# Weight decoding on 513 columns as 27 rows of 19, each VectorE step between touching and gapped rows

## The chip, the cores and the metric

The kernel runs on one core of one Trainium2 chip. The metric is the device time of one execution in microseconds; the figure given for a kernel is the median of its runs. The core has TensorE (PE, with its weight loads shown apart as PEld), VectorE (DVE), ScalarE (ACT), GpSimd (POOL) and SyncE (SP), which issues the transfers here.

## What is computed

The reference is an attention over 4 batches of 8 heads (576 positions, 64 wide) that keeps only the scores within tau of the row's maximum, and then two feed-forward layers on its 2304 x 512 output. The weights of both layers come as float64; they are 512 x 2048 and 2048 x 512.

```python
def _attn_ref(q, k, v, tau):
    scores = scale * np.matmul(q, k.transpose(0, 1, 3, 2))
    thresh = np.max(scores, axis=-1, keepdims=True) - tau
    scores = np.where(scores >= thresh, scores, -1000000000.0)
    scores = scores - np.max(scores, axis=-1, keepdims=True)
    attn = np.exp(scores)
    attn = attn / (np.sum(attn, axis=-1, keepdims=True) + 1e-09)
    return np.matmul(attn, v).astype(np.float32)

def _moe_ref(x, w_in, w_out, alpha):
    h = x @ w_in
    g = np.maximum(h, 0.0) + alpha * np.minimum(h, 0.0)
    return (g @ w_out).astype(np.float32)

def _moe2_ref(x, w_in, w_out):
    h = x @ w_in
    g = h * np.clip(h + 3.0, 0.0, 6.0) / 6.0
    return (g @ w_out).astype(np.float32)
```

## The kernel before, in words

**Attention.** A loop of 144 steps (16 pairs of heads, 9 steps each) runs `do_S` (scores on PE, L361, into the PSUM tile `s`), `soft` (row maximum on DVE, L382; exponential on ACT, L383; threshold and sum on DVE, L385), `soft_norm` (division on POOL, L394), `do_T` (transposes on PE) and `do_PV`. Beside it `prep` splits and transposes the next pair's q and k (`nat`, L102 and L103).

**Feed-forward.** `ffn_groups` makes, for a block of 512 tokens, sixteen `h_group`s (PE L199 into `h`; the nonlinearity in `act1` on DVE L204 and L207, or `act2` on ACT L213 and DVE L215; the high and low part of `g` on ACT L221 and POOL L225) and sixteen `o_group`s (PE L229 or L235, added up on DVE in L487 or L489). Three of the four blocks are queued and dealt out between the attention steps; the last block and a rest of 256 tokens follow at the end.

**Weights.** There are 64 weight chunks of 128 x 512 (16 each of `i1`, `o1`, `i2`, `o2`). Each one is decoded once, in the first block's passes, from float64 to float32, and stored to a scratch in DRAM, from which all later passes load it. A decode is: the load of 512 KB into `raw64` (L125, three buffers); on ACT, the low word scaled to 16 bits (L131, into every second 16-bit place of `low`) and the absolute value of the high word (L132, into `f`); on DVE, the sign and exponent bits taken from 16 bits of the high word (L133, from every fourth 16-bit place of `raw64` into the other places of `low`), a clamp (L135, `f` onto itself) and a shift by 3 (L136, `f` onto itself); on POOL, the sum of `f` and `low` (L137); the store (L138). Then `split` makes the high part on ACT (L102) and the low part on POOL or DVE (L103). Six chunks are decoded early, in the first pair's attention steps; the other 58 come when `ready` asks for them, one chunk ahead of the matmuls that use it.

**Order.** Every engine runs its own queue in order. The queues' order is set by the framework's scheduler when the program is built, from the order in the code, the priorities (`high_priority` for the attention steps) and its own estimates of durations. A change in the instructions can therefore move others.

Of the kernel before, what the change touches and what calls it, by code (L numbers as in the profile page):

```python
# [9 lines left out]
F32 = mybir.dt.float32  # L10
F32R = mybir.dt.float32r
U32 = mybir.dt.uint32
U16 = mybir.dt.uint16
AF = mybir.ActivationFunctionType
ALU = mybir.AluOpType
# [4 lines left out]
P = 128  # L20
NKT = 4


F64_LO = 2.0 ** -15
F64_HI = 122879.9921875


def f32(ap):
    return ap.bitcast(F32)
# [3 lines left out]
def kernel(  # L33
# [13 lines left out]
    nc = tc.nc  # L47
    B, H, S, D = q.shape
    DM = H * D
# [3 lines left out]
    SM = 512  # L53
# [23 lines left out]
    def pool(stack, name, bufs, **kw):  # L77
        return stack.enter_context(tc.tile_pool(name=name, bufs=bufs, **kw))

    const = pool(ctx, "const", 1)  # L80
    stage = pool(ctx, "stage", 4)
# [4 lines left out]
    dec = pool(ctx, "dec", 3)  # L86
# [14 lines left out]
    def split(hi, lo, src, lo_eng):  # L101
        nc.scalar.copy(hi, src)  # L102
        lo_eng.tensor_tensor(out=lo, in0=src, in1=f32(hi), op=ALU.subtract)  # L103
# [3 lines left out]
    wide = moe_w_in.dtype != F32  # L107
    scratch = {}
# [6 lines left out]
    def chunk(nm, ft):  # L115
        w = weights[nm]
        if nm[0] == "i":
            n = w.shape[1] // NF
            return w[:, ft * n:(ft + 1) * n].rearrange("(k p) f -> p k f", p=P)
        return w[ft * P:(ft + 1) * P, :]  # L120

    def decode_load(nm, ft):
        raw = dec.tile([P, DM, 2], U32, tag="raw", name="raw64")
        dst = raw.rearrange("p (k f) a -> p k (f a)", k=NKT) if nm[0] == "i" else raw.rearrange("p n a -> p (n a)")
        nc.sync.dma_start(dst, chunk(nm, ft))  # L125
        return raw

    def decode(nm, ft, raw):
        f = stage.tile([P, DM], U32, tag="st", name="f")
        low = dec.tile([P, DM, 2], U16, tag="low", name="low", bufs=2)  # L130
        nc.scalar.activation(low[:, :, 0], raw[:, :, 0], AF.Copy, scale=2.0 ** -29)  # L131
        nc.scalar.activation(f32(f), f32(raw[:, :, 1]), AF.Abs)  # L132
        nc.vector.tensor_scalar(out=low[:, :, 1], in0=raw.bitcast(U16)[:, :, 3], scalar1=0x8000, scalar2=0x4000,  # L133
                                op0=ALU.bitwise_and, op1=ALU.bitwise_xor)
        nc.vector.tensor_scalar(out=f32(f), in0=f32(f), scalar1=F64_HI, scalar2=F64_LO, op0=ALU.min, op1=ALU.max)  # L135
        nc.vector.tensor_single_scalar(f, f, 3, op=ALU.logical_shift_left)  # L136
        nc.gpsimd.tensor_tensor(out=f, in0=f, in1=low.bitcast(U32).rearrange("p n a -> p (n a)"), op=ALU.add)  # L137
        nc.sync.dma_start(scratch[nm, ft], f32(f))  # L138
        return f32(f)

    raws = {}

    def w_fetch(key, nm, ft, fresh=False):
        if key in raws:
            return
        if wide and fresh:
            raws[key] = decode_load(nm, ft)
            return
        t = stage.tile([P, DM], F32, tag="st", name="st")
        if wide:  # L150
            nc.sync.dma_start(t, scratch[nm, ft])
        elif nm[0] == "i":
            nc.sync.dma_start(t.rearrange("p (k f) -> p k f", k=NKT), chunk(nm, ft))
        else:
            nc.sync.dma_start(t, chunk(nm, ft))
        raws[key] = t
# [12 lines left out]
    def fetch(kind, c):  # L169
        if c < len(passes) * NF and (kind, c) not in ws:  # L170
            nm, ft, _, _, fresh = w_of(kind, c)
            w_fetch((kind, c), nm, ft, fresh)

    def ready(kind, c):
        if c < len(passes) * NF and (kind, c) not in ws:
            fetch(kind, c)
            nm, ft, layer, blk, fresh = w_of(kind, c)
            t = raws.pop((kind, c))
            if wide and fresh:
                t = decode(nm, ft, t)  # L180
            w = (wip if kind == "i" else wop).tile([P, 2, DM], F32R, tag="w" + kind, name="w" + kind)
            if fresh:
                on_dve = layer == 2 and ft % 4 == 3
            else:
                on_dve = ft % 4 < (1 if layer == 1 and blk is not None else 2)
            split(w[:, 0], w[:, 1], t, nc.vector if on_dve else nc.gpsimd)
            ws[kind, c] = w

    def load_x(t, src, n, lo_eng):
        for kt in range(NKT):  # L190
            raw = stage.tile([P, SM], F32, tag="st", name="st")
            nc.sync.dma_start(raw[:, :n], src[kt])
            split(t[:, 0, kt, :n], t[:, 1, kt, :n], raw[:, :n], lo_eng)
        return t
# [57 lines left out]
    for i in range(2):  # L252
        t = a1.tile([P, 2, P], F32R, tag=f"qr{i}", name=f"qr{i}")
# [5 lines left out]
    for i in range(2):  # L259
        t = a1.tile([P, 2, NB + 1, D], F32, tag=f"v{i}", name=f"v{i}")  # L260
# [9 lines left out]
    st = {}  # L270
# [175 lines left out]
    def x_ready(blk):  # L446
        if ("x", 1, blk) not in box:
            box["x", 1, blk] = x0 if blk == 0 else load_x(new_x(), x1d[blk], blocks[blk], nc.gpsimd)
# [73 lines left out]
    def decode_early(n):  # L522
        for nm, ft in early_dec[n - 1:n]:
            decode(nm, ft, raws.pop((nm, ft)))
            decoded.add((nm, ft))
        for nm, ft in early_dec[n:n + 1]:
            w_fetch((nm, ft), nm, ft, True)
# [26 lines left out]
    for i in range(NS):  # L554
        pi, t = divmod(i, NT)
# [4 lines left out]
        if t % 2 == 1 or t == NT - 1:  # L560
            with tc.high_priority(offset=50):
                n = 1 + t % 2
# [6 lines left out]
        while done < min(len(queue), (i + 1 - PB - LAG) * per):  # L569
            f, a = queue[done]  # L570
# [5 lines left out]
    for f, a in queue[done:]:  # L576
# [8 lines left out]
    NBR = blocks[B]  # L585
    LAGO = 2
    xs = {blk: load_x(x2p.tile([P, 2, NKT, blocks[blk]], F32R, tag=f"x{blk}", name="x"), x1d[blk], blocks[blk], nc.vector)
          for blk in (B - 1, B)}
    for layer in (1, 2):
# [6 lines left out]
        for m in range(len(seq) + LAGO):  # L596
            if m < len(seq):
                ft, blk = seq[m]
                n = blocks[blk]
# [11 lines left out]
            ft, blk = seq[m - LAGO]  # L611
            gs = gss.pop(m - LAGO)
            n = blocks[blk]
# [9 lines left out]
            else:  # L623
                for d in range((n + P - 1) // P):
                    o = oa[d] if blk < B else orr[d]
                    mm_o2(o, ws["o", c0 + ft], gs, d, n, first_, last_)
                    if last_:
                        t = ob.tile([P, SM], F32, tag="ob", name="ob")
# [38 lines left out]
```

## Time and profile before

| | us |
|---|---|
| median of 3 runs | 1209.13 (1207.42 to 1209.55) |
| the profiled execution, its own time | 1206.91 |
| span in its profile | 1205.1 |
| PE busy | 1133.9 (94% of the span) |
| POOL busy | 703.9 (58%) |
| DVE busy | 678.6 (56%) |
| ACT busy | 662.8 (55%) |

The profiled execution took 1.8 us more than the span of its profile: that much lies before the first and behind the last instruction. It is 2.2 us below the median of the runs. "Busy" counts the time in which an engine has an instruction under way; instructions of one engine that follow directly can overlap by a few hundredths of a microsecond in the records. Shares of the whole span hide that the stages have different limits, so the profile is best read by stretches of time.

### The profile page before, as it was taken

To read this page: it belongs to the slowest core of one execution; us is meant where nothing else is said; L and a number is where in the kernel's file an instruction comes from. 1 tells how busy PE (TensorE), PEld (TensorE's weight loads), DVE (VectorE), ACT (ScalarE), POOL (GpSimd) and SP (SyncE) were. 2 spreads that over 40 slices of the span, in tenths; PEclk is the share of its full clock that TensorE was granted. 3 is DMA by queue.
4 is the path that set the end of the run, shared out by engine and by line. 5 is a ranking of instruction groups with operands and counts; after the bars stand their busy time and mean duration, and the time that the engine had idled before them with its cause. 6 is when DMAs were issued, how large, how long until landed. Compare 5 with 4: busy or idle time off the path is not lost.

```text
span 1205.1 us, 19458 instructions
## 1 busy us (share of the span) xinstructions
PE 1133.9 (94%) x6944; PEld 939.0 (78%) x6944; DVE 678.6 (56%) x1297; ACT 662.8 (55%) x1272; POOL 703.9 (58%) x710
## 2 busy tenths in 40 slices
PE   5899998888888999999999999999999999999998
PEld 4677786666667787878788878888777888888886
DVE  6877789979979563737254555555235333331221
ACT  6788776757777564546565545445534322243432
POOL 2775788977978775655555665545343443334332
PEclk9899999999899999999999999999999999999999
DMA  6852355475575443242333432232224322212211
GB/s 176 252 151 63 112 175 170 142 208 162 152 243 170 150 147 101 76 120 81 109 86 106 145 107 84 79 103 71 80 79 149 97 61 62 67 57 69 63 36 53
DMA packets 93634, 139.09 MB, mean 115 GB/s; under 512 B 19424, under 2 KB 48608, under 8 KB 93536
## 3 DMA queue, kind: packets, MB, share of 16 engines
q1 hardware_dynamic: 93536, 137.83, 38.9%
q8 instruction: 55, 0.90, 0.3%
q14 instruction: 43, 0.35, 0.1%
HBM read 103.29 MB, written 25.17 MB: 107 GB/s over the span
## 4 chain that ended last, share of the span: by engine, by line
PE 60%; DVE 3%; issue 1%; POOL 1%; DMA 1%; ACT 1%; DVEq 0%; POOLq 0%; ACTq 0%
PE h L199 25%; PE o L235 12%; PE o L229 11%; PE s L361 3%; PE pv L425 3%; PE t L407 2%; PE r L229 2%; PE r L235 2%; DMA st<-wo 1%; DVE m L204 1%; DVE g L207 1%; PE pt L306 1%; POOL wo L103 0%; DVE g L215 0%; PE r L410 0%
## 5 line engine op out<-in xcount | busy, mean ns | idle before, releaser
L199 PE MATMUL h<-x,wi 128*128 128x512 f32 (+1 forms) x1536 | 356.6, 381 | 2.9 <-DVE g L207 1.0
L225 POOL TENSOR_TENSOR gs<-g,gs 128x512 fp32r<-128x512 f32 (+1 forms) x160 | 194.6, 1217 | 220.0 <-ACT gs L221 218.9
L199 PEld LDWEIGHTS h<-x,wi 128*128 128x128 f32 x1536 | 273.7, 189 | 56.7 <-DVE g L207 1.5
L235 PE MATMUL o<-wo,gs 128*128 128x512 f32 x768 | 197.5, 402 | 10.0 <-DVE g L215 7.2
L229 PE MATMUL o<-gs,wo 128*128 128x512 f32 x768 | 196.1, 401 | 9.1 <-DVE g L207 8.1
L235 PEld LDWEIGHTS o<-wo,gs 128*128 128x128 f32 x768 | 142.3, 191 | 43.8 <-DVE g L215 9.8
L229 PEld LDWEIGHTS o<-gs,wo 128*128 128x128 f32 x768 | 141.9, 191 | 41.0 <-DVE g L207 11.7
L215 DVE SCALAR_TENSOR_TENSOR g<-m,h 128x512 f32<-128x512 f32 x80 | 50.3, 630 | 163.2 <-ACT m L213 161.9
L204 DVE TENSOR_SCALAR m<-h,alpha_sb 128x512 f32<-128x512 f32 x80 | 55.5, 694 | 145.8 <-PE h L199 145.6
L221 ACT CAST gs<-g 128x512 fp32r<-128x512 f32 (+1 forms) x160 | 92.8, 580 | 72.1 <-DVE g L207 34.6
L394 POOL TENSOR_SCALAR e<-e,rc 128x576 f32<-128x576 f32 x144 | 116.6, 820 | 25.7 <-DVE rc L391 24.5
L383 ACT ACTIVATE e<-s,nmx 128x576 f32<-128x576 f32 x144 | 107.3, 749 | 43.7 <-DVE nmx L382 43.0
L385 DVE SCALAR_TENSOR_TENSOR e<-s,thr,e 128x576 f32<-128x576 f32 x144 | 115.9, 811 | 18.4 <-ACT e L383 15.1
L382 DVE TENSOR_REDUCE nmx<-s 128x1 f32<-128x576 f32 x144 | 107.2, 750 | 31.6 <-PE s L361 31.2
L103 POOL TENSOR_TENSOR wi<-st,wi 128x512 fp32r<-128x512 f32 x58 | 74.8, 1290 | 79.6 <-ACT wi L102 79.4
L425 PE MATMUL pv<-p,v 128*64 128x128 f32 (+1 forms) x1600 | 109.7, 273 | 9.3 <-DVE g L215 6.7
L361 PE MATMUL s<-ka,qt 128*128 128x288 f32 x512 | 101.1, 323 | 17.0 <-DVE e L385 9.5
L213 ACT ACTIVATE m<-h,three 128x512 f32<-128x512 f32 x80 | 51.3, 644 | 116.1 <-PE h L199 115.8
L102 ACT CAST wo<-st 128x512 fp32r<-128x512 f32 x99 | 59.3, 622 | 91.8 <-DMA st<-wo 75.9
L425 PEld LDWEIGHTS pv<-p,v 128*64 128x64 f32 x1600 | 84.8, 139 | 31.8 <-issue 15.1
L103 POOL TENSOR_TENSOR wo<-st,wo 128x512 fp32r<-128x512 f32 x58 | 77.2, 1347 | 50.7 <-ACT wo L102 50.5
L102 ACT CAST wi<-st 128x512 fp32r<-128x512 f32 x99 | 60.9, 616 | 80.3 <-PE h L199 43.6
(85 smaller groups left out, 1648.8 us busy)
## 6 DMA issues: line engine op xcount, KB each, us to landing
st<-wi SPq DMA_DIRECT2D x99, 256.0 KB, 2.7
st<-wo SPq DMA_DIRECT2D x99, 256.0 KB, 2.7
raw<-in_moe_w_in_dram SPq DMA_DIRECT2D x32, 512.0 KB, 4.4
raw<-in_moe_w_out_dram SPq DMA_DIRECT2D x32, 512.0 KB, 4.0
ka<-ka SPq DMA_DIRECT2D x30, 304.0 KB, 4.3
wi<-f SPq DMA_DIRECT2D x32, 256.0 KB, 3.1
wo<-f SPq DMA_DIRECT2D x32, 256.0 KB, 3.1
raw<-in_k_dram SPq DMA_DIRECT2D x16, 256.0 KB, 3.6
```

The costliest lines, as they stand in the source:

```text
L102: nc.scalar.copy(hi, src)
L103: lo_eng.tensor_tensor(out=lo, in0=src, in1=f32(hi), op=ALU.subtract)
L199: nc.tensor.matmul(h[:, :n], lhsT=w[:, ws, kt * P:(kt + 1) * P], rhs=x[:, xs, kt, :n], start=(i == 0), stop=(i == len(steps) - 1))
L225: nc.gpsimd.tensor_tensor(out=gs[:, 1, :n], in0=g[:, :n], in1=f32(gs[:, 0, :n]), op=ALU.subtract)
L229: nc.tensor.matmul(o[:, :n], lhsT=w[:, ws, dt * P:(dt + 1) * P], rhs=gs[:, gsel, :n], start=fresh and start and i == 0, stop=stop and i == ...
L235: nc.tensor.matmul(o[:m, :], lhsT=gs[:, gsel, tt * P:tt * P + m], rhs=w[:, ws, :], start=start and i == 0, stop=stop and i == 2)
L361: nc.tensor.matmul(ps[:, half, 0:SH], lhsT=w, rhs=s["k"][:, a, c + half * SH:c + half * SH + SH], start=(n == 0), stop=(n == len(mms) - 1))
L382: nc.vector.tensor_reduce(out=nmx, in_=ps, axis=AX.XY, op=ALU.max, negate=True)
L383: nc.scalar.activation(eh, ps, AF.Exp, bias=nmx, scale=1.0)
L385: nc.vector.scalar_tensor_tensor(out=eh, in0=ps, scalar=thr, in1=eh, op0=ALU.is_ge, op1=ALU.mult, accum_out=sm[:, h:h + 1])
L394: nc.gpsimd.tensor_scalar(out=eh, in0=eh, scalar1=rc[:, h:h + 1], scalar2=0.0, op0=ALU.mult, op1=ALU.add)
L425: nc.tensor.matmul(pv[64 * h:64 * h + 64, :], lhsT=vn[:, h, kt, :], rhs=pt[:, blk, c:c + m], start=(kt == 0), stop=(kt == NB), skip_group_ ...
```

## The change

Each decode now works on 513 columns: the 512 of the chunk and one column of padding, seen as 27 rows of 19. The tiles `raw64` and `f` (and with it every tile of the pool `stage`) get 513 columns, in which the 27 rows touch. The tile `low` and a new tile `cl` get 540 columns, of which each row of 20 uses 19, so their rows have a gap. The three DVE steps each go from one kind to the other: L133 (now L151) from `raw64`, touching, to `low`, gapped; the clamp L135 (now L153) from `f`, touching, to `cl`, gapped, where it was from `f` to `f`; the shift L136 (now L154) from `cl`, gapped, back to `f`, touching. The framework writes the touching side as one run of 513. The ACT step L131 (now L149) writes gapped rows, and the POOL sum L137 (now L155) reads them from `low`. The three buffers of `raw64` are now made once, with the padding column set to zero by three small POOL instructions at the start, and taken in turn; transfers still move 512 columns.

```diff
--- before.py
+++ after.py
@@ -119,24 +119,43 @@
             return w[:, ft * n:(ft + 1) * n].rearrange("(k p) f -> p k f", p=P)
         return w[ft * P:(ft + 1) * P, :]
 
+
+
+    RA, RB, RG = 27, 19, 20
+    raw64 = []
+    for i in range(3 if wide else 0):
+        t = const.tile([P, RA * RB, 2], U32, name=f"raw64{i}")
+        nc.gpsimd.memset(t[:, DM:], 0)
+        raw64.append(t)
+
+    def rows(ap):
+        return ap.rearrange("p (a b) -> p a b", a=RA)[:, :, 0:RB]
+
+    def st_tile(dt, name):
+        return stage.tile([P, RA * RB], dt, tag="st", name=name)
+
     def decode_load(nm, ft):
-        raw = dec.tile([P, DM, 2], U32, tag="raw", name="raw64")
-        dst = raw.rearrange("p (k f) a -> p k (f a)", k=NKT) if nm[0] == "i" else raw.rearrange("p n a -> p (n a)")
+        raw = raw64.pop(0)
+        raw64.append(raw)
+        dst = raw[:, 0:DM]
+        dst = dst.rearrange("p (k f) a -> p k (f a)", k=NKT) if nm[0] == "i" else dst.rearrange("p n a -> p (n a)")
         nc.sync.dma_start(dst, chunk(nm, ft))
         return raw
 
     def decode(nm, ft, raw):
-        f = stage.tile([P, DM], U32, tag="st", name="f")
-        low = dec.tile([P, DM, 2], U16, tag="low", name="low", bufs=2)
-        nc.scalar.activation(low[:, :, 0], raw[:, :, 0], AF.Copy, scale=2.0 ** -29)
+        f = st_tile(U32, "f")
+        cl = dec.tile([P, RA * RG], U32, tag="cl", name="cl", bufs=2)
+        low = dec.tile([P, RA * RG, 2], U16, tag="low", name="low", bufs=2)
+        nc.scalar.activation(rows(low[:, :, 0]), rows(raw[:, :, 0]), AF.Copy, scale=2.0 ** -29)
         nc.scalar.activation(f32(f), f32(raw[:, :, 1]), AF.Abs)
-        nc.vector.tensor_scalar(out=low[:, :, 1], in0=raw.bitcast(U16)[:, :, 3], scalar1=0x8000, scalar2=0x4000,
+        nc.vector.tensor_scalar(out=rows(low[:, :, 1]), in0=rows(raw.bitcast(U16)[:, :, 3]), scalar1=0x8000, scalar2=0x4000,
                                 op0=ALU.bitwise_and, op1=ALU.bitwise_xor)
-        nc.vector.tensor_scalar(out=f32(f), in0=f32(f), scalar1=F64_HI, scalar2=F64_LO, op0=ALU.min, op1=ALU.max)
-        nc.vector.tensor_single_scalar(f, f, 3, op=ALU.logical_shift_left)
-        nc.gpsimd.tensor_tensor(out=f, in0=f, in1=low.bitcast(U32).rearrange("p n a -> p (n a)"), op=ALU.add)
-        nc.sync.dma_start(scratch[nm, ft], f32(f))
-        return f32(f)
+        nc.vector.tensor_scalar(out=rows(f32(cl)), in0=rows(f32(f)), scalar1=F64_HI, scalar2=F64_LO, op0=ALU.min, op1=ALU.max)
+        nc.vector.tensor_single_scalar(rows(f), rows(cl), 3, op=ALU.logical_shift_left)
+        nc.gpsimd.tensor_tensor(out=rows(f), in0=rows(f), in1=rows(low.bitcast(U32).rearrange("p n a -> p (n a)")), op=ALU.add)
+        f = f32(f)[:, 0:DM]
+        nc.sync.dma_start(scratch[nm, ft], f)
+        return f
 
     raws = {}
 
@@ -146,7 +165,7 @@
         if wide and fresh:
             raws[key] = decode_load(nm, ft)
             return
-        t = stage.tile([P, DM], F32, tag="st", name="st")
+        t = st_tile(F32, "st")[:, 0:DM]
         if wide:
             nc.sync.dma_start(t, scratch[nm, ft])
         elif nm[0] == "i":
@@ -188,7 +207,7 @@
 
     def load_x(t, src, n, lo_eng):
         for kt in range(NKT):
-            raw = stage.tile([P, SM], F32, tag="st", name="st")
+            raw = st_tile(F32, "st")[:, 0:SM]
             nc.sync.dma_start(raw[:, :n], src[kt])
             split(t[:, 0, kt, :n], t[:, 1, kt, :n], raw[:, :n], lo_eng)
         return t
```

The number of decode instructions on each engine stays the same; the scheduler puts some in another place. On DVE, in the stretch where blocks of the first layer run between attention steps, this is the decode of one chunk (`f_2810` before, `f_2815` now; `e`, `s`, `nmx`, `thr`, `rc` belong to the attention, `acc` to the feed-forward layer). Before:

```order
L385 SCALAR_TENSOR_TENSOR e_3557,sm_3558<-s_3666,thr_3672,e_3557 128x576
L385 SCALAR_TENSOR_TENSOR e_3790,sm_3791<-s_3785,thr_3793,e_3790 128x576
L135 TENSOR_SCALAR f_2810<-f_2810 128x512
L487 TENSOR_TENSOR acc_2041<-o_2679,acc_2041 128x512
L391 RECIPROCAL rc_3678<-den_3677 128x2
L136 TENSOR_SCALAR f_2810<-f_2810 128x512
```

And with the change:

```order
L153 TENSOR_SCALAR cl_2816<-f_2815 128x27x19
L404 SCALAR_TENSOR_TENSOR e_3563,sm_3564<-s_3672,thr_3678,e_3563 128x576
L154 TENSOR_SCALAR f_2815<-cl_2816 128x513
L404 SCALAR_TENSOR_TENSOR e_3796,sm_3797<-s_3791,thr_3799,e_3796 128x576
L410 RECIPROCAL rc_3684<-den_3683 128x2
L506 TENSOR_TENSOR acc_2047<-o_2685,acc_2047 128x512
```

The clamp and the shift now stand ahead of and between the two softmax steps instead of behind them.

On POOL, these are sums of early decodes and the work between them. Before:

```order
L137 TENSOR_TENSOR f_496<-f_496,low_497 128x512
L394 TENSOR_SCALAR e_438<-e_438,rc_463 128x576 x2
L137 TENSOR_TENSOR f_576<-f_576,low_577 128x512
L103 TENSOR_TENSOR nat_364<-raw_261,nat_364 128x9x64
L137 TENSOR_TENSOR f_651<-f_651,low_652 128x512
```

And with the change:

```order
L155 TENSOR_TENSOR f_501<-f_501,low_503 128x513
L409 TENSOR_SCALAR den_467<-sm_444 128x2
L103 TENSOR_TENSOR nat_369<-raw_267,nat_369 128x9x64
L155 TENSOR_TENSOR f_581<-f_581,low_583 128x513
L413 TENSOR_SCALAR e_443<-e_443,rc_468 128x576 x2
```

The sum and the division of the attention (L394, now L413) have changed places. Behind row 498 of some 1,440 on PE the order of the matmuls is that of before.

## Rows read from the trace of the kernel before

**Rows 1.** The page, part 1: busy time of PE over the whole span.

```profile
PE 1133.9 (94%) x6944; PEld 939.0 (78%) x6944; DVE 678.6 (56%) x1297; ACT 662.8 (55%) x1272; POOL 703.9 (58%) x710
```

**Rows 2.** Busy time by stretch: us, engines, clock granted to PE, DMA share, GB/s.

```profile
0.00:30.00 30.00, 17.73 (x99) 14.86 (x99) 20.15 (x54) 20.07 (x37) 8.74 (x18) 1.00 0.61 175
30.00:180.00 150.00, 140.38 (x1117) 113.89 (x1118) 119.72 (x276) 118.96 (x243) 113.29 (x140) 0.97 0.52 150
180.00:390.00 210.00, 175.88 (x1039) 142.30 (x1038) 186.82 (x304) 144.92 (x265) 174.35 (x153) 0.96 0.59 178
390.00:420.00 30.00, 28.30 (x160) 22.54 (x161) 16.93 (x28) 17.92 (x37) 23.36 (x22) 0.94 0.52 164
420.00:1205.00 785.00, 771.58 (x4532) 645.38 (x4530) 335.03 (x638) 360.88 (x695) 384.18 (x380) 1.00 0.30 88
```

**Rows 3.** PE's waits in 180 to 390 us: total, times, longest.

```profile
PE s L361 <- DVE e L385: 7.3, 4, 4.9
PE o L229 <- DVE g L207: 6.9, 4, 3.8
PE pv L425 <- DVE g L215: 6.7, 3, 4.6
PE s L361 <- DVE thr L384: 3.5, 1, 3.5
PE o L235 <- DVE g L215: 2.5, 2, 2.3
```

**Rows 4.** DVE's costliest groups in 180 to 390 us: busy us, mean ns.

```profile
L133 DVE TENSOR_SCALAR low<-raw 128x512 uint16<-128x512 uint16 x42 | 38.2, 910 | 3.9 <-POOL f L137 3.9
L136 DVE TENSOR_SCALAR f<-f 128x512 uint32<-128x512 uint32 x43 | 37.9, 881 | 0.5
L135 DVE TENSOR_SCALAR f<-f 128x512 f32<-128x512 f32 x43 | 36.8, 860 | 7.9 <-ACT f L132 7.9
```

**Rows 5.** The three DVE decode steps, whole run: duration ns min/median/max.

```profile
L133 DVE TENSOR_SCALAR low<-raw x64: 440/588/1659, 22.3 to 402.5; 128x512 uint16<-128x512 uint16 x64
...
L135 DVE TENSOR_SCALAR f<-f x64: 397/740/1720, 24.3 to 409.7; 128x512 f32<-128x512 f32 x64
...
L136 DVE TENSOR_SCALAR f<-f x64: 400/778/1532, 24.8 to 410.2; 128x512 uint32<-128x512 uint32 x64
```

**Rows 6.** DVE alone in order of time, 196 to 216 us: start, duration, instruction.

```profile
197.36 1.51 DVE L136 TENSOR_SCALAR f<-f 128x512 uint32<-128x512 uint32 x1
...
209.79 0.41 DVE L135 TENSOR_SCALAR f<-f 128x512 f32<-128x512 f32 x1
...
212.50 1.24 DVE L133 TENSOR_SCALAR low<-raw 128x512 uint16<-128x512 uint16 x1
```

**Rows 7.** POOL alone over the same time.

```profile
197.10 1.49 POOL L103 TENSOR_TENSOR nat<-raw,nat 128x576 fp32r<-128x576 f32 x1
...
210.89 1.27 POOL L137 TENSOR_TENSOR f<-f,low 128x512 uint32<-128x512 uint32 x1 [1.79 <-ACT low L131]
212.12 1.28 POOL L103 TENSOR_TENSOR wi<-f,wi 128x512 fp32r<-128x512 f32 x1
```

**Rows 8.** DVE steps with an operand in PSUM, 150 to 420 us: duration ns min/median/max.

```profile
L385 DVE SCALAR_TENSOR_TENSOR e<-s,thr,e x35: 792/804/820, 149.5 to 399.6; 128x576 f32<-128x576 f32 x35
...
L215 DVE SCALAR_TENSOR_TENSOR g<-m,h x15: 665/673/689, 300.2 to 418.6; 128x512 f32<-128x512 f32 x15
```

**Rows 9.** A DVE step of two operands in SBUF, whole run: duration ns min/median/max.

```profile
L103 DVE TENSOR_TENSOR wi<-st,wi x41: 666/684/830, 46.1 to 1161.6; 128x512 fp32r<-128x512 f32 x41
```

**Rows 10.** POOL's steps, whole run: duration ns min/median/max.

```profile
L103 POOL TENSOR_TENSOR nat<-raw,nat x30: 1402/1429/1627, 15.2 to 782.5; 128x576 fp32r<-128x576 f32 x30
...
L137 POOL TENSOR_TENSOR f<-f,low x64: 1259/1294/1482, 25.4 to 410.8; 128x512 uint32<-128x512 uint32 x64
...
L394 POOL TENSOR_SCALAR e<-e,rc x144: 741/752/1464, 18.0 to 846.9; 128x576 f32<-128x576 f32 x144
```

**Rows 11.** POOL's division of the attention in 180 to 390 us: busy us, mean ns.

```profile
L394 POOL TENSOR_SCALAR e<-e,rc 128x576 f32<-128x576 f32 x25 | 24.0, 968 | 3.6 <-DVE rc L391 3.5
```

## The prediction

> **What bounds the kernel now.** I read the page first, then the busy time by stretch, then PE's waits in the stretch that stood out, then the DVE steps that the change touches, one by one. Over the whole span PE is busy 94% [rows 1], which looks like a kernel that only PE can shorten. The stretches say more [rows 2]. From 420 us on PE is busy 771.58 of 785 us: nothing that DVE or POOL saves there can be worth more than 13 us, and no decode runs there at all, since the last one starts at 410 us [rows 5]. Between 180 and 390 us PE is busy only 175.88 of 210 us, while DVE is busy 186.82 (89%) and POOL 174.35 (83%). In this stretch 43 of the 64 chunks are decoded [rows 4], and the waits of PE name DVE: the five longest sums come to 7.3 + 6.9 + 6.7 + 3.5 + 2.5 = 26.9 us of PE's 34.1 us of idle time [rows 3], 79%. So DVE sets the pace here. [...]
>
> **What the decode steps cost now.** DVE's three decode steps take 38.2 + 37.9 + 36.8 = 112.9 us in this stretch, 54% of its time [rows 4]. Their means are 860 to 910 ns, but the shortest of them take 397 to 440 ns and the longest 1532 to 1720 ns [rows 5]. The timeline says why. The clamp at 209.79 us began when POOL had nothing to do (POOL's next step starts at 210.89, after 1.79 us of idleness) and took 0.41 us. The shift at 197.36 began 0.26 us into a POOL step that lasts from 197.10 to 198.59; it ended at 198.87, 0.28 us behind that step. The sign step at 212.50 began 0.38 us into a POOL step that ends at 213.40, and ended at 213.74, 0.34 us behind it [rows 6, 7]. So a decode step that begins during a POOL step does its work only when POOL is through. DVE steps that read PSUM show no such thing: 35 threshold steps lie between 792 and 820 ns and 15 steps of `g` between 665 and 689 ns [rows 8], all of them beside a POOL that is busy four fifths of the time. POOL is held up the other way round: its division has a median of 752 ns over the run [rows 10] and a mean of 968 ns here [rows 11].
>
> **The change, part by part.** What it adds is small. Three POOL instructions at the start set two words a partition to zero, before POOL has anything else to do: nothing. One column more in 512 is 1 or 2 ns a step: nothing. Transfers are as they were, from and to 512 columns, and no buffer count falls, so SP's queue gets no new wait; the second tile `cl` only replaces a step onto itself. ACT's and POOL's row gaps I take at nothing too: POOL's split of `nat`, whose output goes in 9 separate rows, takes 1429 ns for 576 columns, 2.48 ns a column, against 1294 / 512 = 2.53 for the sum in one run [rows 10].
>
> What counts is the kind of step. A free step of 512 columns takes 0.40 us, while steps of two operands with the same columns take 673 [rows 8] and 684 ns [rows 9]: the free decode step goes through its columns about two at a time. I take it that it does so by working on two halves at once, and that this is what POOL shuts out. Two halves need the same cut on both sides. Before, 512 columns against 512 columns can be cut at 256. Now one side is a run of 513 and the other 27 rows of 19: half of 27 rows is 13 or 14 rows, 247 or 266 columns, and half of 513 is 256 or 257. No cut fits both, so I take the step to go one column at a time, and not to meet POOL any more. The trace shows no such step from SBUF to SBUF with one operand, so I bound its price. Below, 397 ns (nothing changes, and POOL free); above, 1.5 us (one at a time and still behind POOL). The nearest rows are the steps of 512 columns at 673 and 684 ns: I take 690 for the clamp and the shift. The sign step's free minimum is 40 ns above the others [rows 5], for it reads every fourth 16-bit place; one column at a time I take that twice: 770 ns.
>
> [...]
>
> Sum for 180 to 390 us: the sign step 42 x 0.77 = 32.3, clamp and shift 2 x 43 x 0.69 = 59.3, together 91.6 instead of 112.9: DVE gets back 21.3 us. For the other 21 chunks I count nothing: by the medians of the whole run a decode takes 588 + 740 + 778 = 2106 ns now [rows 5] and 770 + 690 + 690 = 2150 then, and those chunks lie mostly where PE is busy 140.38 of 150 us [rows 2]. How much of 21.3 us becomes time? DVE's saving counts where its queue is full, 89% of the stretch, and where PE's wait ends with DVE, 79% or a little more: 21.3 x 0.89 x 0.8 = 15 us. POOL gets back 25 x (968 - 752) = 5 us on its divisions alone [rows 10, 11], and the clock's 8 us may come back in part as PE waits less; for both I add 1 us. The clamp and shift now stand partly ahead of softmax steps on which the score matmuls wait, 0.69 us each time against a mean of 0.87 before: no loss. So 16 us. Against the profiled execution: 1206.9 - 16 = 1190.9. The median of the runs is 2.2 us above that execution, so the forecast for the median is **1193 us**.
>
> [...]
>
> **The rivals.**
> *The step keeps its two halves.* Then it still waits for POOL, nothing changes but the order of some instructions, and the time is **1209 us**. For it: no row shows how the engine cuts 27 rows against one run. Against it: the halves don't match.
> *One column at a time, and still shut out by POOL.* Slower. If what POOL blocks is any DVE step whose source and destination both lie in SBUF, the step keeps its wait and its own work grows by 0.29 us for clamp and shift and 0.33 us for the sign step: 86 x 0.29 + 42 x 0.33 = 39 us more on DVE, of which by the same shares 28 us show: **1237 us**. It decides from the point at which the mean wait of 0.45 us (910 - 440, 860 - 397) stays. For it: no step with its only source in SBUF shows otherwise. Against it: L215 and L385 write SBUF and read one operand there, and never wait [rows 8].
> *POOL pays for the gaps.* If the sum takes 21.3 / 43 = 0.5 us more for its 27 rows, POOL has all of DVE's gain added to its 174 us and becomes the bound: **1207 us** or a little worse. Against it: the 9 rows of `nat` cost nothing.
> [...]
>
> **How the numbers follow.** About 0.2%, 2.4 us, is what a measurement of this kernel tells from no change. Forecast 0.70, dear sign step 0.12, halves kept 0.08, POOL's gaps 0.05, still shut out 0.05. Faster: 0.70 + 0.12 = 0.82. Within 0.2%: the 0.08 of the kept halves and half of POOL's gaps, 0.11. Slower: the rest, 0.07. The range: at best all 21 us of DVE's saving, the clock's 8 us and a little of POOL's count, 1209 - 31 = 1178; at the upper end the dear sign step with a poorer share, or POOL's gaps, 1207. Left out are the kept halves and the shut-out case, 0.13, and a little beyond the low end.
>
> **What would show it.** [...] The sum (L155) should stay at 1.29 us and POOL's division fall back to 0.75. PE's idle time between 180 us and the last decode should shrink from 34 us to some 20, its clock there rise, and the last decode start near 395 us instead of 410; behind it the stretches should be as long as before. The prediction is wrong in its main step if DVE's decode time doesn't fall, and wrong in its share if it falls by 20 us and the end doesn't move.

## The result and the profile after

The changed kernel takes **1181.33 us** (median of 6 runs, 1178.01 to 1182.13) where the kernel before took 1209.34 us on the same chip (6 runs, 1207.42 to 1210.41). The ratio is 0.9765, with a 95% interval of 0.9754 to 0.9775: 28 us faster. The forecast was 1193 us, with a range of 1178 to 1207. The sign and the range held; the gain is 28 us and not 16.

The page of the changed kernel, parts 1 and 2, says where to look. PE's share has gone from 94% [rows 1] to 96%, and its busy time has fallen by 6.6 us although it runs the same 6944 matmuls.

```profile
span 1179.4 us, 19483 instructions
PE 1127.3 (96%) x6944; PEld 933.8 (79%) x6944; DVE 650.5 (55%) x1297; ACT 663.2 (56%) x1272; POOL 672.9 (57%) x713
...
PE   6789999999999999999999999999999999999998
...
PEclk9899999999999999999999999999999999999999
```

The instructions of the changed kernel by line give each decode step's shortest, median and longest duration in ns (L151 is the sign step, L153 the clamp, L154 the shift, L155 POOL's sum, L413 the division). They answer to [rows 5, 10].

```profile
L151 DVE TENSOR_SCALAR low<-raw x64: 746/771/795, 22.3 to 376.1; 128x513 uint16<-128x513 uint16 x64
...
L153 DVE TENSOR_SCALAR cl<-f x64: 654/677/692, 25.0 to 383.5; 128x513 f32<-128x513 f32 x64
...
L154 DVE TENSOR_SCALAR f<-cl x64: 658/679/691, 26.3 to 384.2; 128x513 uint32<-128x513 uint32 x64
...
L155 POOL TENSOR_TENSOR f<-f,low x64: 1162/1187/1510, 27.1 to 385.0; 128x513 uint32<-128x513 uint32 x64
...
L413 POOL TENSOR_SCALAR e<-e,rc x144: 739/747/1286, 18.0 to 821.1; 128x576 f32<-128x576 f32 x144
```

The spread is the thing to see. Before, a clamp took anything from 397 to 1720 ns; now all 64 clamps lie between 654 and 692. None is as short as the short ones were, and none is long. The last decode's sum starts at 385.0 us instead of 410.8 [rows 10]: 25.8 us earlier, and the span is 25.7 us shorter. So dividing both traces at that instant compares equal work. This is the busy time by stretch ahead of it and behind it, columns as in [rows 2], first of the kernel before:

```profile
0.00:410.80 410.80, 353.08 (x2350) 285.90 (x2350) 339.80 (x654) 296.60 (x567) 313.94 (x326) 0.96 0.56 167
410.80:1205.00 794.20, 780.77 (x4596) 653.06 (x4594) 338.84 (x643) 366.16 (x705) 389.99 (x385) 1.00 0.31 89
```

and then of the changed kernel:

```profile
0.00:385.00 385.00, 346.79 (x2350) 281.08 (x2350) 312.58 (x654) 297.50 (x567) 283.65 (x328) 0.98 0.58 178
385.00:1179.40 794.40, 780.52 (x4596) 652.70 (x4594) 337.94 (x643) 365.66 (x705) 389.20 (x385) 1.00 0.31 89
```

The counts of PE, DVE and ACT agree on both sides, so the division falls at the same place in the program. Behind it nothing changed (794.2 and 794.4 us). Ahead of the last decode DVE's busy time fell by 27.2 us, POOL's by 30.3 us, ACT's not at all. PE's idle time fell from 57.7 to 38.2 us, and its busy time by 6.3 us for the same 2350 matmuls, under a granted clock of 0.98 instead of 0.96: 19.5 + 6.3 = 25.8.

From 180 us to the last decode PE is idle for 14.2 of 205 us at a granted clock of 0.99, where it was idle for 34.1 of 210 us at 0.96 [rows 2]:

```profile
180.00:385.00 205.00, 190.84 (x1154) 155.29 (x1152) 175.14 (x330) 160.52 (x294) 172.57 (x172) 0.99 0.64 200
```

PE's waits in this stretch, which answer to [rows 3], show the same: the three longest sums now come to 6.1 us, where the three longest before came to 20.9.

```profile
PE o L248 <- DVE acc L506: 2.2, 2, 1.2
PE pv L444 <- DVE g L234: 2.0, 1, 2.0
PE o L254 <- DVE g L234: 1.9, 3, 1.1
```

### The profile page after: what moved, and what is told of

It is laid out like the page before. It is cut to its first block, busy times and chain, and to the rows that moved or that the text cites. A ratio compares the mean times of both kernels' runs of the same rounds, so it can differ in the third digit from the quotient of the medians.

```text
span 1179.4 us, 19483 instructions
## 1 busy us (share of the span) xinstructions
PE 1127.3 (96%) x6944; PEld 933.8 (79%) x6944; DVE 650.5 (55%) x1297; ACT 663.2 (56%) x1272; POOL 672.9 (57%) x713
## 4 chain that ended last, share of the span: by engine, by line
PE 63%; DVE 5%; ACT 4%; issue 3%; DMA 2%; POOL 2%; DVEq 0%; ACTq 0%; POOLq 0%; SPq 0%
PE h L218 25%; PE o L254 14%; PE o L248 11%; PE s L380 3%; PE pv L444 3%; PE t L426 2%; PE r L248 2%; PE r L254 2%; DMA st<-wo 1%; DMA raw<-in_moe_w_out_dram 1%; DVE nmx L401 1%; DVE g L226 1%; ACT m L232 1%; POOL wo L103 1%; DVE m L223 1%
## 5 line engine op out<-in xcount | busy, mean ns | idle before, releaser
L244 POOL TENSOR_TENSOR gs<-g,gs 128x512 fp32r<-128x512 f32 (+1 forms) x160 | 191.4, 1196 | 212.7 <-ACT gs L240 211.9
L401 DVE TENSOR_REDUCE nmx<-s 128x1 f32<-128x576 f32 x144 | 107.6, 751 | 30.7 <-PE s L380 30.3
L413 POOL TENSOR_SCALAR e<-e,rc 128x576 f32<-128x576 f32 x144 | 109.3, 770 | 25.6 <-DVE rc L410 23.8
L103 POOL TENSOR_TENSOR wi<-st,wi 128x512 fp32r<-128x512 f32 x58 | 75.0, 1294 | 80.2 <-ACT wi L102 80.0
```

The costliest lines, as they stand in the source:

```text
L244: nc.gpsimd.tensor_tensor(out=gs[:, 1, :n], in0=g[:, :n], in1=f32(gs[:, 0, :n]), op=ALU.subtract)
L401: nc.vector.tensor_reduce(out=nmx, in_=ps, axis=AX.XY, op=ALU.max, negate=True)
L413: nc.gpsimd.tensor_scalar(out=eh, in0=eh, scalar1=rc[:, h:h + 1], scalar2=0.0, op0=ALU.mult, op1=ALU.add)
```

## The experiments

**Four layouts.** The first question was whether the gain really comes from the cut that doesn't fit (theory A), or from the new tiles and gaps themselves. The first experiment keeps the tiles and the gaps but lets both sides be halved:

```diff
-    RA, RB, RG = 27, 19, 20
+    RA, RB, RG = 32, 16, 17
...
-        nc.gpsimd.memset(t[:, DM:], 0)
```

> Rows of 32 x 16 with a pitch of 17 instead of 27 x 19 with a pitch of 20: the same tiles and the same gaps, but 512 against 32 can be halved at the same column, and the order of the instructions on DVE and PE is that of the kernel before. Theory A (the steps change their kind because no cut fits both sides): clamp and shift are again 0.40 us when POOL is idle, with a maximum of 1.5 us, and the time is 1209 us within 3. Theory B (the new tiles, the fixed buffers or the gaps bring the gain): about 1181 us. If gaps in the second operand are what makes POOL's sum faster (1.19 us in the changed kernel against 1.29 before), it is 1.19 us here too, and the time a few us below 1209.

Measured: 1206.44 us against 1210.59 of the kernel before in the same session, a ratio of 0.9967 (0.9951 to 0.9982). Clamp (L152), shift (L153) and sum (L154) of this kernel:

```profile
L152 DVE TENSOR_SCALAR cl<-f x64: 394/636/1509, 24.5 to 411.0; 128x512 f32<-128x512 f32 x64
...
L153 DVE TENSOR_SCALAR f<-cl x64: 399/781/1527, 24.9 to 411.4; 128x512 uint32<-128x512 uint32 x64
...
L154 POOL TENSOR_TENSOR f<-f,low x64: 1182/1202/1622, 25.5 to 412.0; 128x512 uint32<-128x512 uint32 x64
```

The short and the long steps are back. In the two traces every engine runs its instructions in the same order as in the kernel before, so this comparison is free of the scheduler. Tiles, fixed buffers and gaps are not the cause of the 28 us. With the shorter sum that comes with the gaps they are worth 4 us.

The second keeps the 513 columns and takes the gaps away (`RA, RB, RG = 27, 19, 19`), so that both sides of every step have the same odd count:

> 513 columns as in the change, but no gaps anywhere: 513 against 513 on every DVE step. Theory A: both sides can be cut at the same column, so the steps keep two halves and their waits: minimum 0.40 us, maximum over 1.4 us, time 1209 us within 4. Rival (an odd count alone makes a step go one column at a time): minimum 0.68 us and about 1181 us. POOL's sum: 1.29 us if gaps make it faster, 1.19 us if the odd length does.

Measured: 1212.5 us, ratio 1.0009 (0.9997 to 1.002), no change. The clamp and the sum:

```profile
L153 DVE TENSOR_SCALAR cl<-f x64: 405/737/1640, 24.5 to 411.8; 128x513 f32<-128x513 f32 x64
...
L155 POOL TENSOR_TENSOR f<-f,low x64: 1267/1298/1611, 25.5 to 412.8; 128x513 uint32<-128x513 uint32 x64
```

An odd count on both sides changed nothing: the clamp still takes 405 to 1640 ns. Of the layouts tried, only 513 in one run against 27 rows, both odd and unequal, changes the kind; an odd count against an even one was not tried. And the sum is back at 1298 ns, so its gain comes from the gaps in its second operand, not from the length (1202 ns with gaps at 512 columns, 1298 without at 513).

The third and the fourth make one half of the change each.

```diff
-        low = dec.tile([P, RA * RG, 2], U16, tag="low", name="low", bufs=2)
+        low = dec.tile([P, RA * RB, 2], U16, tag="low", name="low", bufs=2)
```

> Gaps only in the tile between clamp and shift; the low words touch. Theory A: clamp and shift 0.68 us with no long ones, the sign step as before (minimum 0.44, mean 0.8 to 0.9 us). DVE gets back some 20 of the 24 us of its decode time, and the time falls by two thirds of the gain or more: 1187 to 1193 us. If the gain is the sum's shorter duration on POOL, most of it stays away: above 1198 us.

```diff
-        cl = dec.tile([P, RA * RG], U32, tag="cl", name="cl", bufs=2)
+        cl = dec.tile([P, RA * RB], U32, tag="cl", name="cl", bufs=2)
```

> Gaps only in the low words; clamp and shift go from touching rows to touching rows. Theory A: the sign step 0.77 us with no long ones, clamp and shift as before (0.40 to 1.5 us, mean 0.83). A third of the gain or less: 1197 to 1206 us. If the sum's shorter duration on POOL (1.19 us for a gapped second operand) is the gain: below 1192 us.

Measured: 1191.79 us (ratio 0.9837, 0.9822 to 0.9851) with clamp and shift of the new kind, and 1198.98 us (0.9894, 0.9876 to 0.9912) with the sign step of the new kind and the shorter sum. The groups of instructions by line (busy us, mean ns), first of the kernel with the gapped clamp, show which step had changed its kind:

```profile
L151 DVE TENSOR_SCALAR low<-raw 128x513 uint16<-128x513 uint16 x64 | 59.3, 929 | 9.1 <-POOL f L155 5.1 <-DMA raw<-in_moe_w_out_dram 2.1 <-DMA raw<-in_moe_w_in_dram 1.8
L154 DVE TENSOR_SCALAR f<-cl 128x513 uint32<-128x513 uint32 x64 | 43.3, 678 | 0.7 <-issue 0.5
L153 DVE TENSOR_SCALAR cl<-f 128x513 f32<-128x513 f32 x64 | 43.2, 677 | 11.8 <-ACT f L150 11.8
```

and then of the one with the gapped low words:

```profile
L154 DVE TENSOR_SCALAR f<-cl 128x513 uint32<-128x513 uint32 x64 | 51.2, 803 | 1.5
L153 DVE TENSOR_SCALAR cl<-f 128x513 f32<-128x513 f32 x64 | 51.2, 802 | 14.7 <-ACT f L150 14.5
L151 DVE TENSOR_SCALAR low<-raw 128x513 uint16<-128x513 uint16 x64 | 49.2, 770 | 3.1 <-POOL f L155 1.9 <-DMA raw<-in_moe_w_in_dram 1.2
```

Against all rows touching (1212.5 us) the halves bring 20.7 and 13.5 us, together 34.2, and the whole change 31.2: nearly additive, about 10 us for a step, and some 4 for the sum. The changed kernel was measured in another session than these four; the kernel before took 1208.6 to 1210.6 us from session to session, so differences from the changed kernel, here and below, are good to about 2 us. The order of the instructions differs between these kernels too.

**The order held still.** The scheduler orders the queues by its own estimates of time, and in the changed kernel it ordered them otherwise. To see the kind without the order, both kernels were built with the scheduler's estimates of time off:

```diff
-    with _tile.TileContext(nc, schedule_with_timeline_sim=True) as tc:
+    with _tile.TileContext(nc, schedule_with_timeline_sim=False) as tc:
```

> The kernel before, with the framework's estimates of durations switched off when it orders the queues: the order then doesn't depend on which kind of step it believes in. It serves as the base of the next run; its time itself isn't forecast (other order, perhaps 1200 to 1300 us). Decode steps 0.40 to 1.5 us as in the kernel before.

> The changed kernel in the same way: DVE's order is now instruction for instruction that of the run before it, and PE's and POOL's differ in under 0.3% of the rows. Theory A (the kind of step brings the gain): 20 us or more below the run before it. Theory B (a good part of the gain comes from the other order): less than 14 us below it.

Measured: 1379.19 us and 1362.06 us (ratios to the kernel before 1.1406, 1.1382 to 1.143, and 1.1276, 1.1242 to 1.131). With DVE's order the same instruction for instruction the change is worth 17 us, between the two numbers that the theories had named. ACT's order is the same too, POOL's but for the three small instructions at the start, and PE's but for 4 of 6944 matmuls. This order is 14% slower and leaves the steps more room: before the change the clamp's mean is 641 ns there instead of 839. These are part 1 of the page and the clamp's group, first before the change:

```profile
PE 1236.9 (90%) x6944; PEld 967.3 (70%) x6944; DVE 662.8 (48%) x1297; ACT 677.8 (49%) x1272; POOL 691.8 (50%) x710
...
L135 DVE TENSOR_SCALAR f<-f 128x512 f32<-128x512 f32 x64 | 41.0, 641 | 21.6 <-ACT f L132 20.8
```

and then with it:

```profile
PE 1230.5 (90%) x6944; PEld 962.0 (71%) x6944; DVE 668.7 (49%) x1297; ACT 679.4 (50%) x1272; POOL 672.8 (49%) x713
...
L153 DVE TENSOR_SCALAR cl<-f 128x513 f32<-128x513 f32 x64 | 43.5, 682 | 22.3 <-ACT f L150 22.0
```

DVE's busy time goes up by 6 us here, and its three decode steps take 136.4 us instead of 129.7. So the 17 us are not DVE's time: POOL's busy time falls by 19 us, 8 us of it in the sum (84.1 to 76.0). In this order the largest sum of PE's waits, over the whole run, names POOL's division (before the change: us in total, times, longest):

```profile
PE t L407 <- POOL e L394: 56.2, 47, 3.7
```

The pair shows that the new steps and the faster sum together gain without a change of order, and without a gain of time on DVE. It doesn't part the steps from the sum. How much of the 28 us the new order adds in the tuned kernel stays open.

**Fillers in the wrong place.** To measure what a microsecond of each engine is worth, one more step per decode was added to the changed kernel, on a tile of its own:

```diff
+    fsrc = const.tile([P, RA * RB], F32, name="fsrc")
+    fdst = const.tile([P, RA * RG], F32, name="fdst")
...
+        nc.vector.tensor_scalar(out=rows(fdst), in0=rows(fsrc), scalar1=F64_HI, scalar2=F64_LO, op0=ALU.min, op1=ALU.max)
```

> The changed kernel with one more DVE step per decode that nobody waits for, on a tile of its own, from touching to gapped rows: 64 x 0.68 = 44 us of DVE work of the kind that goes one column at a time. If DVE paces the stretch, 0.7 to 1 of it shows: 1211 to 1225 us. If after the change PE or POOL paces it: under 1200 us.

> The same filler on 512 columns without a gap, the kind with two halves: 0.40 us of own work, 26 us in all instead of 44. Theory A: it waits for POOL (mean near 0.8 us, maximum 1.5) and POOL waits for it (the division's mean over 0.80 again), so it costs more than the filler of one column at a time, although its own work is 0.28 us less. If waits between DVE and POOL don't matter: it costs less, 18 us or so.

> The changed kernel with one more POOL step per decode that nobody waits for (one operand, 512 columns, about 0.68 us by the division's 0.75 us for 576): 64 x 0.68 = 44 us on POOL. If POOL's relief is as much the cause of the gain as DVE's: 25 us or more above the changed kernel. If DVE alone paces the stretch: under 10 us above it.

> The changed kernel with one more ACT copy of 512 columns per decode that nobody waits for (0.62 us, 40 us in all). ACT is busy 78% in the stretch 180 to 362 us. If only DVE and POOL pace it: under 10 us above the changed kernel; if the four engines hold each other: 15 us or more.

Measured: 1200.85 us (0.9938, 0.9923 to 0.9953), 1192.38 us (0.9865, 0.985 to 0.988), 1182.97 us (0.9781, 0.9763 to 0.9799) and 1186.98 us (0.9819, 0.9802 to 0.9837): 20, 11, 2 and 6 us above the changed kernel. The forecasts of the first two were missed, and the second seems to speak against theory A. The filler's own row, first in the kernel whose filler goes from touching to gapped rows, tells why:

```profile
L160 DVE TENSOR_SCALAR fdst<-fsrc x64: 662/677/689, 2.1 to 124.6; 128x513 f32<-128x513 f32 x64
```

and in the kernel whose filler has 512 columns without a gap:

```profile
L160 DVE TENSOR_SCALAR fdst<-fsrc x64: 400/420/1567, 2.1 to 104.5; 128x512 f32<-128x512 f32 x64
```

A step that waits for nothing is put at the front by the scheduler: all 64 began before 125 us, ahead of the crowded stretch, and half of those without a gap took 420 ns or less, near their shortest of 400. These four runs say nothing about the stretch, POOL's and ACT's least of all.

**Fillers in the right place.** The last two runs let the filler read the clamped tile, so that it can't run before its decode. Both read the same 513 columns; they differ only in whether the rows of the destination touch or have the same gap as the source:

```diff
+        nc.vector.tensor_scalar(out=rows(fdst[:, 0:RA * RB]), in0=rows(f32(cl)), scalar1=F64_HI, scalar2=F64_LO, op0=ALU.min, op1=ALU.max)
```

> The changed kernel with one more DVE step in every decode that nobody waits for. It reads the clamped tile, so it stands where the decodes stand; the earlier fillers read a constant tile and all ran before 125 us, ahead of the stretch they were meant for. It goes from gapped to touching rows: 64 x 0.68 = 44 us of DVE work. If a microsecond of DVE shows as one at the end: about 44 us above the changed kernel; by the share of 0.71 that the prediction took: 31 us; by the share that the early filler showed (0.45): 20 us.

```diff
+        nc.vector.tensor_scalar(out=rows(fdst), in0=rows(f32(cl)), scalar1=F64_HI, scalar2=F64_LO, op0=ALU.min, op1=ALU.max)
```

> The same step, same place, same 513 columns, but from gapped to gapped rows: 27 against 27, which can be cut at the same row. Theory A: 0.40 us when POOL is idle, up to 1.5 us else, mean 0.75 to 0.9 us beside decodes, and POOL's division longer again (mean over 0.78), so the time is as far above the changed kernel as with the step of one column at a time or farther. If only a step's own work counts: 0.6 of the other's cost.

Measured: 1201.92 us (0.9945, 0.9926 to 0.9964) and 1209.62 us (1.0, 0.9983 to 1.0017): 20.6 and 28.3 us above the changed kernel. The filler and POOL's sum of the first kernel, from its groups by line, and the filler's shortest, median and longest duration:

```profile
L157 POOL TENSOR_TENSOR f<-f,low 128x513 uint32<-128x513 uint32 x64 | 75.7, 1187 | 19.2 <-ACT p L430 5.5 <-issue 5.0 <-DVE f L156 4.8
L158 DVE TENSOR_SCALAR fdst<-cl 128x513 f32<-128x513 f32 x64 | 43.5, 680 | 0.0
...
L158 DVE TENSOR_SCALAR fdst<-cl x64: 666/678/703, 26.9 to 408.0; 128x513 f32<-128x513 f32 x64
```

and of the second:

```profile
L157 POOL TENSOR_TENSOR f<-f,low 128x513 uint32<-128x513 uint32 x64 | 79.6, 1248 | 29.8 <-DVE f L156 9.3 <-ACT e L405 6.0 <-issue 5.7
L158 DVE TENSOR_SCALAR fdst<-cl 128x513 f32<-128x513 f32 x64 | 48.8, 762 | 0.0
...
L158 DVE TENSOR_SCALAR fdst<-cl x64: 416/705/1645, 27.0 to 415.3; 128x513 f32<-128x513 f32 x64
```

Here the runs agree with theory A: the step whose shortest took 0.42 us takes 762 ns on average and up to 1645, POOL's sum becomes 61 ns longer, and the kernel loses 8 us more than with the step that always takes 0.68 us (666 to 703 ns). One part was missed: POOL's division stayed at 768 ns, where over 780 had been expected; it is the sum that paid. One such filler step takes back the whole gain of three changed steps.

## Why the prediction was right, and where it was short

**The kind of step.** Right, and in size too: 690, 690 and 770 ns were taken, 677, 678 and 771 are the measured means, and no step is long any more (the maxima are 692, 691 and 795 ns). The reason given, that no cut fits both sides, passed its tests: in the layouts tried, counts that are equal or both even keep the short and long steps (all touching, 513 on both sides, 405 to 1640 ns for the clamp; even gaps, 512 against 32 rows, 394 to 1509 ns; and the last filler with 27 rows on both sides, 416 to 1645 ns); 513 against 27 rows changes them. That the short step works on two halves at once, with one cut for both sides, stays an assumption of the prediction: the runs show durations, not how the engine goes through its columns. The first rival, kept halves, is out: with it a step that meets no POOL would still take about 0.40 us [rows 5], and the minima are 654 and 658 ns.

**What shuts the step out.** The second rival, one column at a time and still behind POOL, is out by the maxima of 692 and 795 ns, beside a POOL that was busy 172.57 of 205 us between 180 us and the last decode.

**POOL's gaps.** The third rival was wrong in sign: the sum became faster, 1187 ns instead of 1294.

**The sign step.** Its median is 771 ns, where 770 had been taken. The "dear sign step", with its chance of 0.12 and its place at the upper end of the range, no run shows: all 64 sign steps lie between 746 and 795 ns. The step reads every fourth 16-bit place and writes every second one; it takes 94 ns more than the clamp, 0.18 ns a column.

**DVE's saving.** 21.3 us were forecast for 180 to 390 us. With the measured means, 42 x 0.771 + 43 x (0.677 + 0.678) = 90.6 us instead of 112.9 [rows 4], it is 22.3, and 24 us over all 64 decodes. "For the other 21 chunks I count nothing" was off by 2 us.

**The share: the step that failed.** The prediction turned 21.3 us of DVE into 15 us by "89% of the stretch" times "79% or a little more", and gave POOL and the clock "1 us" together. The price of DVE's time and the 1 us for POOL were both mis-sized. A microsecond of plain DVE work in this place shows as 20.6 / 43.5 = 0.47 us, less than 0.71; by that, 24 us of DVE's time would be 11 us. The rest, 17 us, is more than the busy time tells. This price is of a step that nobody waits for, in the changed kernel; what a microsecond of a decode step was worth in the fuller queue of before, no run shows. But with the order held still the kernel gained 17 us while DVE's busy time grew, so the gain isn't DVE's time alone. The sum of the parts fits without being a proof: to swap the filler for the kind that always takes 0.68 us is worth 28.3 - 20.6 = 8 us for 64 steps (2 us either way by the spread of their runs), three steps make 23 (6 us either way), and with the 4 us of gaps and sum it is 27, against 28 measured. So the step that exchanges waits with POOL cost this kernel more than DVE's record of it: the last filler took 5.3 us more of DVE's time than the one before it (48.8 against 43.5) and 8 us more at the end. It held POOL too, whose sum took 1248 ns on average with it instead of 1187. With the change POOL's busy time up to the last decode fell by 30.3 us, where the prediction had seen 5 us of divisions. By line, over the run: the sum 9.3 us (85.5 to 76.2), the division 7 us (116.6 to 109.3); the rest is spread over POOL's other steps. Not all of it is held time: by the medians, 64 x (1294 - 1187) = 7 us of the sum's part come with the gaps. The clock's 8 us in the prediction's sum and range no run shows; what the two traces show is 6.3 us less of PE's busy time up to the last decode, for the same 2350 matmuls, at a granted clock of 0.98 instead of 0.96. How the 17 us divide between POOL's held time, the faster sum, the uncertainty of a step's length in an order that was planned for one length, and the new order itself, no run here separates.

**The end.** "Behind it the stretches should be as long as before" held to 0.2 us, and "the last decode start near 395 us instead of 410" became 385. PE's idle time between 180 us and the last decode shrank to 14.2 us, where some 20 had been forecast: the steps worked as foreseen, and more of PE's waits went with them.

## What to carry to other kernels

A fast step can be the dearer one (28.3 us for the filler of 0.42 to 1.65 us, 20.6 for the one of 0.68): look at the spread of one line's durations, and where the shortest and the longest differ by a factor of four beside a busy POOL (397 and 1720 ns for the clamp of before), ask what a slower step that never waits would cost. Here 0.68 us always beat 0.40 us sometimes, and a layout with unequal odd counts on the two sides, 513 against 27, was enough to choose it. Read the gain off the engine that shared the waits too: with the order held still it was POOL's busy time that fell, and DVE's that rose. When you add a filler to price an engine, tie it to the place you mean and read its start times: a step without a dependency runs wherever the scheduler likes (here all 64 began before 125 us).

## What the runs showed of the hardware that was not expected

POOL's sum of two operands of 512 or 513 columns in SBUF takes, in the six layouts without a filler, 1294 to 1298 ns (median) when both lie in one run, and 1187 to 1202 ns when the second operand lies in rows with a gap, 27 x 19 at a pitch of 20 or 32 x 16 at a pitch of 17. The gaps of the low words alone decide it (1190 with gaps there and nowhere else, 1296 with gaps elsewhere). ACT, which writes those gapped rows, pays for them: its step from the raw word takes 832 ns (median) in the changed kernel and with even gaps, 799 with all rows touching. Why POOL gains was not tried.
